# Local attention followed by a Fourier mix and an MLP: another load order, batch 1 on the later batches' path, batch 0's reversed copies taken from PSUM

## The chip, the cores and the metric

The kernel runs on one core of a Trainium2 chip. The metric is device time in microseconds (us); a run's time is that of the one core. The profile is one execution recorded by the hardware profiler. PE is TensorE (matmuls), PEld its weight loads, DVE is VectorE, ACT is ScalarE, POOL is GpSimd, SP is SyncE, whose queue issues most DMAs.

## The reference

Inputs are q, k, v of shape (4 batches, 8 heads, 768 positions, 64), and two weight matrices, 512 x 2048 and 2048 x 512, all float32. Cut to what matters:

```python
scores = q @ k^T / 8 + bias          # bias = -slope[h] * distance
keep   = (pos < 8) | (0 <= rel < 96) # 8 global columns, a local band of 96
a      = softmax(where(keep, scores, -1e9));  attn = a @ v
x      = attn.transpose(0, 2, 1, 3).reshape(4, 768, 512)
u      = x + real(fft(fft(x, axis=1), axis=2))
un     = (u - mean) / sqrt(var + 1e-6)
out    = u + relu(un @ w_ch1) @ w_ch2
```

## The kernel before

The four batches pass through the same stages; a head pair `hp` (two heads of 64, 128 lanes) is the unit of attention.

**Attention.** `load` brings q, k and v of a pair to SBUF as float32 (384 KB each). `cast_qk` or `cast_direct` makes them float16. `trans` turns q and k by TensorE transposes into a PSUM tile `pt` and evacuates it to `qkT` (L521); `trans_dma` does it by DMA transposes instead. `score` computes three groups `g` of score tiles per pair. In batches 0 and 1 a matmul of the constant distance table against a scaled identity `sid` (L542, L547) first puts the bias into the PSUM bank, the score matmuls (L552) are added to it, and ScalarE's exponential (L575) is the weight. In batches 2 and 3 there is no bias matmul: ScalarE writes the exponential to `er` (L572), and VectorE multiplies it by a table `mk` (L587), which ScalarE computes once from the distances (L1128). v takes two paths as well: in batches 0 and 1 it is cast (`cast_v0`, L414), and `v_place` permutes its rows with small matmuls (`pvp`, L427) and copies the result out of PSUM (L443, L444); in batches 2 and 3 the load itself permutes the rows (two DMAs, L336) and POOL casts once (`cast_v`, L454). `FB = 2` is the first batch of the later path. The eight global columns go through `kG` (small POOL copies of `qkT`, L481), `v_global`, `glob`, and `av` adds all into `pav`, which VectorE normalizes into `x` (L699, L700).

**Mix.** `bounce` writes `x` to DRAM and reads it back in another row order as `xr` (L719, L727). The Fourier transform is folded: sums and differences on VectorE (`fold_3` for batch 0, `fold_s` and `fold_d` for the others) into `zy`, `eA`, `ww`; then `y_unit` (matmuls `py`, L881; copies to `zy`, L896, L898), `mirror` (POOL copies of `zy` with reversed order, L916 to L918 into `rev`, L929 into `ww`), and `u_unit` (matmuls `pu`, L961; VectorE adds `xr` and accumulates the row sum, L980; L984 scales that sum; L995 and L997 normalize the mean away). `nt_unit` transposes the result (`ptu`, L1025) and copies it to `unT`. ScalarE's squares (L1004) and POOL's power (L1011, L1012) give the deviation.

**MLP.** Per chunk of 256 rows (12 chunks), `ph_unit` does eight groups of the first product (L1053) with a Relu to `hT` (L1059, L1060), and `pg_unit` the second product (L1076), whose result VectorE adds to `u` (L1085) before the store (L1090).

**The order of the work** comes from a planner, class `Plan`, which runs while the program is built. Each engine has a clock, each operation a cost in us, a list of what it needs and a rank. TensorE takes from four streams (`MIX`, `ATT`, `PH`, `PG`) the unit that can start first; `later` puts other operations in a list, and the one that can start first is written out, lower rank first. The engines run the queues so written in order.

**Buffers and gates.** `buf` hands out rotating SBUF tiles, and `free` names the release that the next user waits for. q and k of batch 1 are staged in the tiles of w1 and w2, so both weights load only when these casts are done: `wload` issues eight POOL DMAs (L1164, L1169), each a quarter of w1 or w2 with a cast to float16. `hold`, a 4-byte DMA on SP that reads the last quarter of w2 (L1178), holds back batch 2's loads. Batches 0 and 1 may use two more pairs of PSUM banks, `C` and `D`; `ph` and `pg` use that space afterwards, so `ph_unit` needs the token `CD`, given when all of batch 0's units with a choice of banks, and those of batch 1 that took `C` or `D`, are done:

```python
needs = [("unT", c), ("w1", jp // 2)] + (free("hT", 5 + c) if jp == 0 else []) + [("CD",)]
```

Of the kernel before, what the change touches and what calls it, by code (L numbers as in the profile page):

```python
# [14 lines left out]
P = 128  # L15


class Plan:
# [10 lines left out]
    def __init__(self):  # L29
        self.t = {"PE": 0.0, "ACT": 0.0, "DVE": 0.0, "POOL": 0.0, "SP": 0.7, "DMA": 1.9, "DMA2": 0.0}  # L30
        self.tok = {}
        self.ready = []
        self.pending = []
        self.rings = {}
        self.left = {}
        self.n = 0
# [49 lines left out]
    def emit(self, place):  # L86
# [6 lines left out]
        if dma:  # L93
            q = "DMA2" if eng == "ACT" or outs and outs[0][0] in ("xw", "xr") else "DMA"
# [82 lines left out]
def kernel(  # L177
# [23 lines left out]
    FB = 2  # L201
    DB = 1
    assert (B, H, S, Dh, NG, NL) == (4, 8, 768, 64, 8, 96)
# [66 lines left out]
    def bank(tag, name, dtype=FP32):  # L270
# [4 lines left out]
        if "late" not in early:  # L275
# [6 lines left out]
            "ww": 1, "rev0": 1, "u": 4, "un": 2, "unT": 2, "w1": 1, "w2": 1}  # L282
# [36 lines left out]

    def load(b, hp, which):  # L320
        n = HP * b + hp
        h0 = 2 * hp
        gate = [("gate",)] if n == FB * HP else []
        if b >= FB:
            srcs = [(0, q), (1, k)] if which == "qk" else [(2, v)]
            for w, src in srcs:
                i = 2 + 3 * (n - FB * HP) + w

                def run(src=src, i=i, w=w):
                    t = stage[("t", n, w)] = buf("qs", i, [P, 2 * NS, Dh], FP32, 1)  # L330
# [6 lines left out]
                pl.later([("SP", 0.55 if w < 2 else 1.1, run)], free("qs", i) + gate, 0.0, [("ld", n, w)], lat=1.7, dma=2.67)  # L337
                if w < 2:
                    cast_direct(b, hp, w, i)
# [5 lines left out]
        else:  # L345
            tag, ti, users, slot = (("hT", hp, 2, 0) if hp < 3 else ("qs", 0, 1, None)) if b == 0 else \
                (("w1", "w2")[hp // 2], 0, 4, 2 * (hp % 2))
            for w, src in enumerate((q, k)):
                at = (tag, ti) if slot is not None else (tag, w)

                def run(w=w, src=src, at=at):
                    if slot is None:
                        t = buf(at[0], at[1], [P, NS, 2 * Dh], FP32, 1)
                    else:
                        if at not in stage:
                            stage[at] = buf(at[0], at[1], [P, users, NS, 2 * Dh], FP32, users)
                        t = stage[at][:, slot + w]
                    stage[("t", n, w)] = t
# [16 lines left out]
    def cast_qk(b, hp, w, at):  # L375
# [9 lines left out]
        if b == 0 and not (w and hp):  # L385
            ways.append(("DVE", dve2(768), lambda: cast("DVE")))
        elif b == 0:
            ways = [("POOL", 0.87, lambda: cast("POOL"))]
        else:
            ways.append(("POOL", 0.87, lambda: cast("POOL")))  # L390
        pl.later(ways, [("ld", n, w)] + free("qk", n), 0.0, [("qk", n, w)], [("free",) + at], rank=b)

    def cast_direct(b, hp, w, i):
# [895 lines left out]
```

## Time and profile before

| what | before |
|---|---|
| time, median of 3 runs | 279.25 us (278.58 to 280.61) |
| the profiled execution's own time | 280.46 us |
| its span | 278.7 us |
| PE busy | 258.7 us, 93% |
| DVE busy | 157.9 us, 57% |
| ACT busy | 148.0 us, 53% |
| POOL busy | 60.8 us, 22% |
| mean granted clock of PE | 0.999 |
| read from and written to HBM | 31.92 MB, 9.44 MB |

The span is what the profile covers; the time of the same execution is 1.76 us longer. Busy time is that in which at least one instruction of the engine runs. Matmuls overlap, and the profile models their ends, so a busy PE need not be at its peak rate. In the timeline a line gives start, duration, engine, source line, operation, output<-input, count, and in brackets the idle time before it with what ended it.

### The profile page before, as it was taken

The page shows a single profiled execution, that of the slowest core. Times are in us where ns is not written, and L with a number is a line of the kernel's source. Part 1 is how long each engine was busy: PE and PEld are TensorE (multiplying, and loading weights), DVE is VectorE, ACT ScalarE, POOL GpSimd, SP SyncE. Part 2 cuts the span into 40 slices and gives each one's busy share as a digit, 9 for nine tenths or more (in the row PEclk, how much of TensorE's full clock was granted, in tenths as well). Part 3 has the DMA queues.
Part 4 walks back from the last instruction along what each step waited for, and adds up shares of the span by engine and source line. Part 5 has one row for each costly group of instructions (what it writes and reads, how often), then busy time and mean ns, then how long its engine had stood idle before and what let it go on. Part 6 is the DMA issues. An engine that isn't in the chain of part 4 may idle for free.

```text
span 278.7 us, 6005 instructions
## 1 busy us (share of the span) xinstructions
PE 258.7 (93%) x2448; PEld 173.2 (62%) x2448; DVE 157.9 (57%) x323; ACT 148.0 (53%) x255; POOL 60.8 (22%) x127
## 2 busy tenths in 40 slices
PE   1999789598789999999999999999999999999994
PEld 1445538458657874677486466777866677767441
DVE  4347781985786414766278968666896661111121
ACT  1466675495666642797782237889242256434000
POOL 1435365931002512412110021401001320100000
PEclk9999999999999999999999999999999999999999
DMA  7999999997774498978858895200164020110122
GB/s 206 290 291 257 339 304 196 207 204 119 194 204 144 105 167 162 231 137 165 196 146 196 214 263 104 66 2 0 40 136 168 1 78 1 40 38 22 56 75 75
DMA packets 70301, 40.69 MB, mean 146 GB/s; under 512 B 27394, under 2 KB 66306, under 8 KB 70274
## 3 DMA queue, kind: packets, MB, share of 16 engines
q1 hardware_dynamic: 61474, 29.83, 43.6%
q0 software_dynamic: 4224, 4.19, 9.3%
q10 hardware_dynamic: 4576, 6.29, 8.3%
q8 instruction: 19, 0.31, 0.5%
q14 instruction: 8, 0.07, 0.1%
HBM read 31.92 MB, written 9.44 MB: 148 GB/s over the span
## 4 chain that ended last, share of the span: by engine, by line
PE 81%; DVE 8%; ACT 4%; issue 2%; DMA 2%; POOL 1%; ACTq 1%; SPq 0%; DVEq 0%; POOLq 0%
PE pg L1076 29%; PE ph L1053 29%; PE py L881 5%; PE sc L552 4%; PE pav L680 3%; PE pu L961 3%; ACT ex L575 2%; PE pt L515 2%; DVE qkT L521 2%; PE ptu L1025 2%; DMA ident<-idm 2%; PE sc L547 2%; PE pav L669 1%; PE sc L542 1%; DVE sm L984 1%
## 5 line engine op out<-in xcount | busy, mean ns | idle before, releaser
L1053 PE MATMUL ph<-unT,w 128*128 128x256 f16 x768 | 93.8, 273 | 2.2 <-DVE hT L1060 2.2
L1076 PE MATMUL pg<-w,hT 128*128 128x512 f16 x384 | 89.9, 379 | 0.0
L1053 PEld LDWEIGHTS <-w 128*128 128x128 f16 x768 | 72.7, 98 | 18.4 <-issue 6.1
L1059 ACT ACTIVATE hT<-ph 128x512 f16<-128x512 f32 x73 | 43.6, 597 | 48.1 <-PE ph L1053 46.9
L1076 PEld LDWEIGHTS <-hT 128*128 128x128 f16 x384 | 36.8, 98 | 36.3 <-issue 0.4
L1085 DVE SCALAR_TENSOR_TENSOR u<-pg,sm,u 128x512 f32<-128x512 f32 x24 | 18.0, 750 | 53.7 <-PE pg L1076 53.5
L575 ACT ACTIVATE ex<-sc 128x992 f16<-128x992 f32 (+2 forms) x24 | 21.3, 925 | 15.1 <-PE sc L552 11.1
L1060 DVE TENSOR_SCALAR hT<-ph 128x512 f16<-128x512 f32 x23 | 15.9, 690 | 11.5 <-PE ph L1053 11.5
L572 ACT ACTIVATE er<-sc 128x992 f16<-128x992 f32 (+2 forms) x24 | 21.5, 923 | 1.6 <-PE sc L552 1.6
L1011 POOL TENSOR_SCALAR sm<-sm 128x2 f32<-128x2 f32 x12 | 3.2, 264 | 71.9 <-ACT un L1004 71.7
L929 POOL COPY ww<-zy 128x512 f16<-128x512 f16 x16 | 9.4, 613 | 42.4 <-PE py L881 42.4
L980 DVE SCALAR_TENSOR_TENSOR u<-pu,xr 128x512 f32<-128x512 f32 x24 | 15.6, 688 | 4.7 <-PE pu L961 4.0
L552 PE MATMUL sc<-qkT 64*128 64x256 f16 (+1 forms) x192 | 17.8, 275 | 0.2 <-DVE qkT L521 0.2
L369 ACT ACTIVATE qk<-qs 128x384 f16<-128x384 f32 (+1 forms) x31 | 14.5, 528 | 6.1 <-DMA qkT<-qk 4.8
L587 DVE TENSOR_TENSOR ex<-er,mk 128x992 f16<-128x992 f16 (+2 forms) x24 | 15.2, 645 | 3.8 <-ACT er L572 3.6
L995 ACT ACTIVATE un<-u,sm 128x512 f16<-128x512 f32 x12 | 8.5, 716 | 16.1 <-DVE sm L984 13.0
L680 PE MATMUL pav<-v,ex 128*128 128x65 f16 x352 | 16.4, 193 | 0.4 <-ACT ex L575 0.4
L680 PEld LDWEIGHTS <-ex 128*128 128x128 f16 x352 | 15.1, 97 | 1.8 <-issue 1.1
L552 PEld LDWEIGHTS <-qkT 64*128 64x128 f16 x192 | 6.0, 96 | 16.1 <-issue 13.2
L896 ACT ACTIVATE zy<-py 128x512 f16<-128x512 f32 (+1 forms) x10 | 8.1, 810 | 14.7 <-PE py L881 14.7
L1004 ACT ACTIVATE un<-un 128x512 f16<-128x512 f16 x24 | 14.8, 620 | 1.5 <-PE ptu L1025 1.4
L898 DVE CAST zy<-py 128x512 f16<-128x512 f32 (+1 forms) x9 | 8.3, 927 | 10.5 <-ACT zy L896 6.4
(101 smaller groups left out, 305.8 us busy)
## 6 DMA issues: line engine op xcount, KB each, us to landing
out_dram<-u SPq DMA_DIRECT2D x24, 256.0 KB, 2.2
w<-in_moe_w_ch_dram POOLq DMA_DIRECT2D x8, 512.0 KB, 11.8
qs<-in_q_dram SPq DMA_DIRECT2D x9, 384.0 KB, 4.7
qs<-in_k_dram SPq DMA_DIRECT2D x9, 384.0 KB, 5.4
u<-in_v_dram SPq DMA_DIRECT2D x8, 384.0 KB, 7.7
xr<-xd ACTq DMA_DIRECT2D x4, 768.0 KB, 4.3
qs<-in_v_dram SPq DMA_DIRECT2D x16, 192.0 KB, 3.9
w<-in_q_dram SPq DMA_DIRECT2D x4, 384.0 KB, 7.5
```

What stands on the lines that cost most here:

```text
L552: nc.tensor.matmul(pa[:, s, c0:c0 + cw], TT[n][lo:lo + 64, 1, i * P:(i + 1) * P], TT[n][lo:lo + 64, 0, i * P:i * P + cw], start=(b > 1), s ...
L572: A(mine(), cut(pa), AF.Exp, 0.0, 0.125)
L575: A(cut(expst[hp][:, :, g * 512:g * 512 + (384 if g == 2 else 512)]), cut(pa), AF.Exp, 0.0, 0.125)
L587: VT(o, mine(), m, op=ALU.mult)
L680: nc.tensor.matmul(po[:, jj, hh * 65:(hh + 1) * 65], lhsT, v16[b % 2][:, i, h, 0:65], start=(jp == 0 and a == 0), stop=(a == len(ops) - 1) ...
L980: V.scalar_tensor_tensor(u[:, a].rearrange("p (n r) -> p n r", r=4), pu[:, a].rearrange("p (r n) -> p n r", r=4), 1.0, XR[b][:, rr].rearra ...
L1004: A(x, x, AF.Square, accum_out=MV[c][:, a, 2:3])
L1053: nc.tensor.matmul(ph[:, a * CH:(a + 1) * CH], W1[0][:, d, jb * P:(jb + 1) * P], UNT[c][:, d, :], start=(d == 0), stop=(d == ND - 1))
L1059: pl.later([("ACT", act(512), lambda: A(dst, ph, AF.Relu)), ("DVE", dve(512), lambda: V.tensor_scalar_max(dst, ph, 0.0))], [], e, [("h", c ...
L1060: ("DVE", dve(512), lambda: V.tensor_scalar_max(dst, ph, 0.0))],
L1076: nc.tensor.matmul(pg, HT[c][:, jb, t * P:(t + 1) * P], W2[0][:, jb, :], start=(jb == 0), stop=(jb == NJ - 1))
L1085: V.scalar_tensor_tensor(UT[c][:, t, :], pg, MV[c][:, t, 3:4], UT[c][:, t, :], op0=ALU.mult, op1=ALU.add)
```

## The change

Batch 1 takes the path of batches 2 and 3 (`FB = 1`) for its v and its scores; its q and k are still transposed by TensorE (`PT`). The loads are ordered: batch 0, five loads of batch 1 (`EARLY`), w1, the rest of batch 1 after batch 0's bounce (token `xi`), then w2, whose tile stages q and k of batch 1's pairs 0 and 1. w1 waits for the cast of batch 1's first q (`W1AT`), its third quarter for the second write of the bounce. Batch 2's loads wait for the third quarter of w2 (`WG`) in place of the last. Batch 0's bounce is issued by SP. The tables `mk` are computed at the start. `kG` is copied from PSUM by the engine that evacuates `pt`, in batches 0 and 1. The reversed copies of batch 0 (`turn`) and the two special rows of every batch (`back`) are made from PSUM by ACT or DVE; POOL keeps the four larger copies of batches 1 to 3. Batch 0's scaling of the row sum goes from DVE to ACT. `C` and `D` are for batch 0 alone.

```diff
-    FB = 2
+    FB = 1
     DB = 1
+    WG = 2
+    W2AT = 1
+    MKA = 4
+    EARLY = [(4, 0), (4, 1), (4, 2), (5, 0), (5, 1)]
+    W1AT = ("qk", 4, 0)
+    PT = (0, 1, 2, 3)
...
+    order = [(n, w) for n in range(HP, B * HP) for w in range(3) if n >= HP + 2 or w == 2]
+    def place(n, w):
+        return ("qs", 2 + order.index((n, w))) if (n, w) in order else ("w2", 0)
...
-                pl.later([("SP", 0.55 if w < 2 else 1.1, run)], free("qs", i) + gate, 0.0, [("ld", n, w)], lat=1.7, dma=2.67)
+                pl.later([("SP", 0.55 if w < 2 else 1.1, run)], free(*at) + gate + [("xi",)] * (b == 1 and (n, w) not in EARLY), 0.0, [("ld", n, w)], lat=1.7, dma=1.47 if w < 2 else 2.3)
...
     def BANKS(b):
-        return ("xx", "C", "D") if b < 2 else ("xx",)
+        return ("xx", "C", "D") if b == 0 else ("xx",)
...
+    def kg_now(b, hp, on, pt):
+        for s in range(2):
+            c0 = 16 * (hp % 2) + 8 * s
+            d = kG[b % 2][64 * s:64 * s + 64, hp, c0:c0 + NG].rearrange("p (t m) -> p t m", t=2)
+            x = pt[64 * s:64 * s + 64, 1, 0:P].rearrange("p (t m) -> p t m", t=2)[:, :, 0:NG // 2]
+            copy_on(on, d, x)
...
-        if b >= FB:
+        if b > FB or b == FB and hp not in PT:
             return trans_dma(b, hp)
...
+            def evac(on):
+                TT[n] = buf("qkT", n, [P, 2, S], FP16, 4)
+                copy_on(on, TT[n], pt[:, :, 0:S])
+                kg_now(b, hp, on, pt)
...
-            if b < 2:
+            if b == 0:
                 for s in range(2):
                     lhsT = sid[:, 2 * hp + s, :]
...
-    XT = [("x", 0), ("hT", 4), ("x", 1), ("x", 2)]
+    XT = [("x", b) for b in range(B)]
...
-        on, eng = "ACT", nc.scalar
+        on, eng = ("ACT", nc.scalar) if b else ("SP", nc.sync)
...
+            def back(on):
+                d = T[("y", b)][:, 7]
+                s0 = py[:, 0, :].rearrange("p (a c m) -> p a c m", a=2, c=2)
+                copy_on(on, d[:, 0, :, 0:1], s0[:, 0, :, 0:1])
+                copy_on(on, d[:, 0, :, 1:P], s0[:, 0, :, P - 1:0:-1])
+                copy_on(on, d[:, 1], s0[:, 1, :, ::-1])
...
+            def turn(on, t):
+                d = REV[0][:, 2 * g + t]
+                copy_on(on, d.rearrange("p a c m -> p (a c) m"), py[:, t, :].rearrange("p (x m) -> p x m", m=P)[:, :, ::-1])
...
-                V.tensor_scalar_mul(sm[:, :, 1], sm[:, :, 0], -SC / Dm)
+                if b:
+                    V.tensor_scalar_mul(sm[:, :, 1], sm[:, :, 0], -SC / Dm)
+                else:
+                    A(sm[:, :, 1], sm[:, :, 0], AF.Copy, 0.0, -SC / Dm)
...
-            pl.later([("ACT", 2 * act(NM), m)], [("c", "dist"), ("x", 1, 3, 2)], 0.0, [("mk", hp)], rank=3)
+            pl.later([("ACT", 2 * act(NM), m)], [("c", "dist")] + [("ex", 0, 3, 2)] * (hp >= MKA), 0.0, [("mk", hp)], rank=2)
...
-            needs = [("vc", 5), ("free", "w1", 0)] if i == 0 else [("wl", 3), ("free", "w2", 0)] if i == 4 else [("wl", i - 1)]
+            needs = [W1AT] if i == 0 else [("wl", 3), ("free", "w2", 0), ("v", 1, W2AT)] if i == 4 else [("wl", i - 1)] + [("xw", 0, 1)] * (i == 2)
...
-            nc.sync.dma_start(g, W2[0][0:1, NJ - 1, 0:2])
-        pl.later([("SP", 0.45, hold)], [("w2", 3)], 0.0, [("gate",)])
+            nc.sync.dma_start(g, W2[0][0:1, 4 * WG, 0:2])
+        pl.later([("SP", 0.45, hold)], [("w2", WG)], 0.0, [("gate",)])
...
-                    if b == 1:
-                        v_place(b, hp)
...
-            mirror(b)
+            if b >= DB:
+                mirror(b)
```

## The prediction

> **What bounds the kernel now.** I read the page's busy line and its 40 slices first, then the busy time of the engines in four stretches that I cut at events of TensorE (PE): its first matmul (6.17), the first score of batch 1 (33.41), the first `ph` matmul (64.33), the end of the last visible wait (98).
>
> ```profile
> PE 258.7 (93%) x2448; PEld 173.2 (62%) x2448; DVE 157.9 (57%) x323; ACT 148.0 (53%) x255; POOL 60.8 (22%) x127
> ...
> PE   1999789598789999999999999999999999999994
> ```
> ```profile
> 6.17:33.41 27.24, 25.07 (x301) 13.00 (x302) 15.89 (x40) 16.19 (x21) 10.91 (x21) 1.00 1.14 290
> 33.41:64.33 30.92, 25.90 (x339) 17.10 (x337) 22.45 (x47) 21.40 (x36) 19.28 (x31) 1.00 1.13 235
> 64.33:98.00 33.67, 31.05 (x324) 25.46 (x321) 21.12 (x40) 20.77 (x39) 5.51 (x10) 1.00 0.62 153
> 98.00:274.70 176.70, 176.67 (x1498) 117.69 (x1496) 95.44 (x185) 88.36 (x159) 24.08 (x57) 1.00 0.46 107
> ```
>
> Columns: stretch, its length, busy PE, PEld, DVE, ACT, POOL, clock, DMA, GB/s. From 98 on PE has no gap, and the clock is full. So the 278.7 us are 6.2 us before the first matmul, 258.7 of PE work, a tail of 4.0 after 274.7, and three idle sums: 2.2, 5.0 and 2.6 (9.8 together). The end moves only by PE work removed or by these 9.8 us growing or shrinking. The second stretch matters most; its PE timeline:
>
> ```profile
> 37.61 0.58 PE L547 MATMUL sc<-dist,sid 128*128 128x496 f16 x2
> 38.12 0.39 PE L552 MATMUL sc<-qkT 64*128 64x256 f16 x4
> ...
> 49.64 0.53 PE L427 MATMUL pvp<-er,ident 64*64 64x128 f16 x24
> ...
> 54.75 0.62 PE L1025 MATMUL ptu<-ident,un 128*128 128x128 f16 x8 [2.50 <-ACT un L995]
> ...
> 60.32 1.07 PE L961 MATMUL pu<-t,ww 128*128 128x128 f16 x16
> ...
> 64.33 1.03 PE L1053 MATMUL ph<-unT,w 128*128 128x256 f16 x8
> ```
>
> The reader is to see that batch 0's last `pu` runs at 60.32, 11.7 us after its last `py` matmul (48.66). `ph` may start only when that `pu` has left its PSUM bank. DVE and POOL say why it is so late:
>
> ```profile
> 51.16 2.78 DVE L984 TENSOR_SCALAR sm<-sm 128x2 f32<-128x2 f32 x1
> ```
> ```profile
> 53.84 0.92 POOL L1169 DMA_DIRECT2D w<-in_moe_w_ch_dram x1
> 54.76 0.84 POOL L414 CAST er<-u 128x768 f16<-128x768 f32 x1
> 55.53 0.62 POOL L929 COPY ww<-zy 128x512 f16<-128x512 f16 x1
> ```
>
> A 2-element operation took 2.78 us while POOL issued w2 and copied (11 others: 0.17), and POOL's reversed copies stood behind weight issues and casts.
>
> **The change, part by part.**
>
> *PE work removed.* Batch 1 loses its bias matmuls. One head pair's three run from 37.61 to 38.12, 38.44 to 38.95 and 39.74 to 40.16: 0.51 + 0.51 + 0.42 = 1.44 us, four pairs 5.8. Lower bound by streaming alone: 2 x (496 + 480 + 384) columns at the rate of `ph` (8 x 256 columns in 0.87 us, 0.425 ns a column) is 1.16, four pairs 4.6. I take 5.8, because batch 2's score without bias takes 0.31 to its successor (122.40 to 122.72), as the plain part does here. `v_place` of batch 1 goes: 0.46 + 0.29 + 0.29 = 1.0. Transposes stay on PE. Sum: 6.8 (5.6 at least), PE work 251.9.
>
> *What comes ahead of the first `ph`.* All 6.8 us lay before 64.33, where PE had 25.07 + 25.90 = 51.0 us of work; 44.2 are left. The removed work was also filler while batch 0's chain ran elsewhere, so it pays only if `ph` moves up. Earliest start T: the last x ends at 34.95; folds until 38.82; 60 `py` matmuls of 0.111 us (6.6) until 45.5. Then three `pu` and three pairs of u additions (6 x 0.69 on DVE from 1.15 us after the last `py`), 5.7 us to the last: T = 51.2. This needs the reversed copies by then. They go to ACT and DVE, straight from PSUM: four of 512 elements (nearest row, the straight copy L898, 0.69; POOL needed 0.61 from SBUF; if reversed reading doubled it, 1.4) and `back` (row L700, 256 elements 0.42, twice, plus a small one: 1.0). Batch 0's scaling L984 goes to ACT, about 0.2 us (nearest row there, 128x1, 0.19), out of POOL's way.
>
> *DVE's additions before T.* Twelve multiplications by `mk` at 0.645 (row L587, 128x992 etc.): 7.7. Sixteen small `kG` copies from PSUM: not in the trace; between 0.06 (a 128x1 memset) and 0.37 (L609 on ACT, 32x256), I take 0.16 as of L1151 (32x4 from PSUM): 2.6. Turns 2.8, `back` 1.0. Removed: four L443 (0.63) 2.5, three L984 0.5. Net 11.1 if DVE takes everything. In 33 to 64 DVE was idle 30.9 - 22.5 = 8.5 us, in 6 to 33 11.4, and ACT shares copies and turns. Cover exists, but a started multiplication holds batch 0's next step up to 0.65. I charge 2 of the 11.1; bounds 0 and 11.1.
>
> *ACT.* The eight `mk` exponentials (0.67 apart) move from 74 to the start: 5.4 us into a stretch where ACT idles 11.0. Each pair can hold one score's exponential by 1.3 at most, and PSUM has banks in reserve. Batch 0's bounce leaves ACT's queue: issues of 1.88, 1.26 and 0.35, of which 1.18 stood on the chain of waits at 27.42. Batch 1's casts become two of 0.518 for one of 0.845: at most 8 x 0.19 = 1.5. Together I charge +0.8 (bounds -1.2 and +4). So T = 51.2 + 2 + 0.8 = 54.0.
>
> *Queues.* SP gets the bounce's five DMAs. Its xr read waits there for the write to land (5.8 us median), and behind it stand seven loads of batch 1 (ten DMAs, since a v is two): from about 35 + 1.3 + 5.8 + 0.4 = 42.5, against 37 before. At 290 GB/s their 2.75 MB take 9.5 us, the second half of w1 beside them two chunks of 2.6 (512 KB at the 204 GB/s of that stage): landed by about 57. Pairs 2 and 3 of batch 1 wait for that, and with them its global part and av. POOL's third w1 issue waits for the bounce too, and its casts of batch 1 stand behind it. Half of w1 is issued at about 26 and needs up to 13 us; the other half by 55.5, when `ph` needs it at T + 3.5. w2 follows by about 67.5 (69.5 before), covered by 24 `ph` groups x 0.87 = 20.9 us from T. The four v loads of batch 1 turn from one 384 KB DMA into two of 192 KB; SP's two issues of such a v took between 1.3 and 4.6 us (L336), a plain one 0.4 to 2.6. Nothing on SP before 64 is nearer than that to PE; it is in the 57.
>
> The Trainium skill, "DMA: Bandwidth & Descriptors", "Why small descriptors are slow (HBM only)", puts the loss at 256-byte descriptors at 27%, which speaks against this v path: by it the four loads would take an estimated 1.5 us more of DMA time, and T or the filler would be that much later at worst. The trace has such loads only in a quiet stage (landing 3.9 us), so no row shows it.
>
> *Weight issues against DVE.* Row: L984 lost 2.6 us to a run of POOL work with four issues, 0.65 each. Chunks 0 to 3 now stand in batch 0's stage: 0 to 2.6, inside the charge of 2 above.
>
> The Trainium skill, "SBUF — State Buffer", "Who interferes with whom", says that GpSimd and a DVE instruction in a two-port mode exclude each other for a whole instruction. It speaks against w1 beside batch 0's attention; by it and the 0.75 us of an issue the estimate would be 4 x 0.75 = 3.0, and the forecast 0.4 later.
>
> *Sum.* Work that can be late: of the 44.2, pairs 2 and 3 (two transposes 1.35, six scores 1.8, global 0.7, av 1.9) = 5.7. So PE has done W = 38.5 to 44.2 at T; middle 41.4. Idle before `ph`: 54.0 - 6.2 - 41.4 = 6.4, against 7.2 now. After it I keep 2.6. Span: 6.2 + 251.9 + 6.4 + 2.6 + 4.0 = 271.1. The profiled execution took 280.46, its span and 1.76 around it; the median of the runs is 279.25, the span and 0.55. So 271.1 + 0.55 = **271.6**. From 98 on, batches 2 and 3 are untouched and I charge nothing: PE is covered there by backlog; if that were gone, each missing us would count fully.
>
> **Rivals.**
> *No pay-off:* filler leaves, data of batch 1 come late, `ph` starts at 60. Idle 60 - 6.2 - 41.4 = 12.4; span 277.1, time 277.6. For it: SP's wait and 235 GB/s in that stretch. Against: w1 no longer waits for batch 1.
> *Full gain:* T near 52 with all 44.2 done leaves the 2.2 of the first stretch, and 0.7 later: 265.0, time 265.5. For it: each larger wait there has a cause that the change touches. Against: late loads.
> *Slower:* DVE becomes the bound of the head. All 11.1 stand before batch 0's steps, T = 62.3, and as batch 1 waits in the same line W is 38.5: idle 17.6, span 282.3, time 282.8. It is slower from T = W + 20.2 on (58.7 here), where the extra idle eats the 6.8. For it: DVE had 11.4 of 14 us busy from 28 to 42. Against: 8.5 idle us after 33, and ACT as a second taker.
>
> **How the numbers follow.** Forecast 0.60 (its own range 267 to 276: T = 52 with W = 44.2, where the first stretch's 2.2 remain, to T = 58 with W = 41.4), no pay-off 0.17, full gain 0.12, slower 0.11. The range runs from T = 51.2 with W = 44.2 and no later idle (264.8) to just past no pay-off, 278.5. About 1%, so 276.5 to 282, is what a measurement tells from no change. Faster: 0.58 of the forecast, the 0.12, and 0.03 of no pay-off, 0.73. Within 1%: 0.02, 0.14 and 0.01 of the slower case, 0.17. Slower: 0.10.
>
> **What would show it.** Right: no L547 or L542 in batch 1, PE busy near 252, first `ph` near 54, last `pu` of batch 0 within 4 us of its last `py`, no DVE operation of 2 elements near 3 us before it. Wrong: PE busy above 254, first `ph` after 58, a new wait of PE above 2 us for a load of batch 1, for `mk` or for a multiplication, or gaps after 98.

## The result and the profile after

The changed kernel takes 293.25 us in the median of four runs (292.73 to 293.70), against 278.91 us of the kernel before on the same chip (278.48 to 280.61). The ratio is 1.0502, with a 95% interval of 1.0451 to 1.0552: **5% slower, 14.3 us**, where the prediction said 271.6 us and at most 278.5. (Ratios here and below leave out runs more than 1.5% above the fastest of the same kernel, in e16 three of five and in e14 two of four, the profiled ones among them, so a ratio can be lower than that of the medians.) The profiled execution took 293.7 us, its span is 291.9 us, 13.2 more than before.

From the profile's page, the busy line of the engines, TensorE's 40 slices and its granted clock:

```profile
PE 259.9 (89%) x2376; PEld 173.1 (59%) x2376; DVE 167.3 (57%) x350; ACT 151.8 (52%) x277; POOL 45.8 (16%) x90
...
PE   1899589651999995899999999999999999999994
...
PEclk9999969895799999999999999999999999999999
```

TensorE has 72 matmuls fewer, and yet its busy time grew from 258.7 to 259.9 us. The clock row says why: some slices stand at 5 to 8 tenths. The windows view of the changed kernel, cut at its first `ph` (56.09), the end of the wait after it (72.50), and the two ends of the thin stretch after 100 (columns as in the prediction):

```profile
5.96:34.45 28.49, 25.05 (x301) 13.02 (x302) 17.78 (x55) 20.76 (x32) 9.19 (x11) 1.00 1.20 282
34.45:56.09 21.64, 16.52 (x176) 12.93 (x177) 16.75 (x37) 16.37 (x32) 4.80 (x7) 0.84 0.95 194
56.09:72.50 16.41, 7.31 (x61) 5.63 (x59) 4.28 (x9) 4.51 (x11) 1.75 (x3) 0.71 1.19 209
72.50:105.00 32.50, 32.50 (x327) 23.91 (x326) 25.48 (x47) 23.90 (x46) 6.28 (x10) 0.94 0.86 184
105.00:126.00 21.00, 17.02 (x157) 11.67 (x156) 11.09 (x24) 11.28 (x24) 6.54 (x13) 1.00 1.02 201
126.00:288.00 162.00, 161.51 (x1365) 105.97 (x1363) 89.30 (x173) 73.68 (x136) 16.24 (x39) 1.00 0.33 83
```

Length less PE busy gives TensorE's idle time: 3.4 and 5.1 us before the first `ph`, 9.1 in the third stretch, 4.0 in the fifth, 0.5 after. In the third stretch ScalarE, VectorE and TensorE are idle together (4.5, 4.3 and 7.3 busy us of 16.4), while the DMA engines are busy all along: everything waits for loads. Three lines of TensorE's timeline:

```profile
56.09 3.46 PE L1082 MATMUL ph<-unT,w 128*128 128x256 f16 x16
59.83 1.91 PE L1082 MATMUL ph<-unT,w 128*128 128x256 f16 x16
...
71.61 3.57 PE L1082 MATMUL ph<-unT,w 128*128 128x256 f16 x16 [9.10 <-ACT hT L1088]
```

The same sixteen matmuls take 1.91 us at full clock and about 3.5 at half. The bracket names what ended the wait of 9.10 us: a copy of `hT` on ScalarE. But a Relu of 0.6 us can't be late by itself, and the chain of waits over this stretch (start, duration, what) shows what stood ahead of it:

```profile
47.00 6.75 DMA qs<-in_k_dram
53.75 16.36 DMA qs<-in_q_dram
70.11 0.02 issue
70.14 0.94 ACT qk L382 x2
71.07 0.49 ACT hT L1088
71.56 0.04 issue
71.61 3.57 PE ph L1082 x16
```

The load of q of batch 1's pair 3, issued at 53.75, landed 16.36 us later. Its cast had been put into ScalarE's queue ahead of the evacuation of `ph`, and ScalarE took its queue in order: the `ph` matmuls that this copy evacuates had ended by 61.8, and the copy came at 70.98, right behind the cast. TensorE stood behind that evacuation. The last loads of batch 1 landed later still: k of pair 3 at about 72.6, and its V was cast at 74.48.

The load was issued so late for two reasons. One is in SyncE's waits (line, waited for, us in total, times, longest), the other in the timelines of SyncE and POOL:

```profile
SPq L742 <- DMA xd<-x: 8.1, 1, 8.1
```

```profile
47.00 2.15 SPq L378 DMA_DIRECT2D qs<-in_k_dram  x1
52.35 1.31 SPq L354 DMA_DIRECT2D qs<-in_v_dram  x2
53.75 0.60 SPq L378 DMA_DIRECT2D qs<-in_q_dram  x1
```

```profile
51.49 0.83 POOL L464 CAST v<-qs 128x768 f16<-128x768 f32 x1 [15.98 <-DMA qs<-in_v_dram]
```

SyncE holds the read of the bounce (L742) for 8.1 us until the write has landed, and q and k of pairs 2 and 3, with V from pair 1 on, stand behind it; in the kernel before all eight q and k loads of batch 1 were issued by 28 us. And in the changed kernel the loads behind the bounce share three rotating `qs` tiles. V of pair 2 uses the tile of pair 1's V, so its issue at 52.35 waited 3.1 us until that V had landed and POOL had cast it, and pair 3's q stood behind it in the queue. The kernel before had a place for each q and k in the tiles of w1 and w2.

**The account.** Clock loss is the sum, over windows of one us, of busy time times one less the granted clock; busy time less that is the work at full clock. This split is rough: the eleven kernels below with the same 2376 matmuls show between 248.6 and 253.7 us of work by it.

| us | before | after | difference |
|---|---|---|---|
| ahead of the first matmul | 6.2 | 6.0 | -0.2 |
| PE work at full clock | 258.7 | 253.3 | -5.4 |
| clock loss | 0.0 | 6.6 | +6.6 |
| idle between first and last matmul | 9.8 | 21.9 | +12.0 |
| tail | 4.0 | 4.2 | +0.2 |
| span | 278.7 | 291.9 | +13.2 |

So the work went away nearly as forecast, as far as this split can tell, and 18.6 us of idle time and half clock came in its place.

### The profile page after: what moved, and what is told of

The parts are those of the page before. It is cut to its first block, busy times and chain, and to the rows that moved or that the text cites. A ratio compares the mean times of both kernels' runs of the same rounds, so it can differ in the third digit from the quotient of the medians.

```text
span 291.9 us, 5881 instructions
## 1 busy us (share of the span) xinstructions
PE 259.9 (89%) x2376; PEld 173.1 (59%) x2376; DVE 167.3 (57%) x350; ACT 151.8 (52%) x277; POOL 45.8 (16%) x90
## 4 chain that ended last, share of the span: by engine, by line
PE 67%; DMA 18%; ACT 5%; DVE 5%; SPq 2%; issue 1%; ACTq 0%; DVEq 0%
PE ph L1082 27%; PE pg L1105 24%; DMA qs<-in_q_dram 8%; DMA xd<-x 5%; PE sc L567 3%; PE pav L695 3%; DMA qs<-in_k_dram 2%; PE py L897 2%; PE pu L992 2%; PE pt L529 2%; DVE x L715 2%; DMA dist<-distm 2%; DMA out_dram<-u 1%; PE ptu L1054 1%; ACT qk L382 1%
## 5 line engine op out<-in xcount | busy, mean ns | idle before, releaser
L1082 PE MATMUL ph<-unT,w 128*128 128x256 f16 x768 | 97.5, 279 | 9.2 <-ACT hT L1088 9.1
L587 ACT ACTIVATE er<-sc 128x992 f16<-128x992 f32 (+2 forms) x36 | 32.9, 923 | 8.8 <-PE sc L567 6.3
L1089 DVE TENSOR_SCALAR hT<-ph 128x512 f16<-128x512 f32 x25 | 17.2, 690 | 22.7 <-PE ph L1082 22.7
L602 DVE TENSOR_TENSOR ex<-er,mk 128x992 f16<-128x992 f16 (+2 forms) x36 | 23.8, 662 | 8.8 <-ACT er L587 8.8
L382 ACT ACTIVATE qk<-qs 128x384 f16<-128x384 f32 x38 | 17.5, 517 | 16.6 <-DMA qs<-in_q_dram 15.3
L464 POOL CAST v<-qs 128x768 f16<-128x768 f32 x12 | 10.2, 849 | 74.4 <-DMA qs<-in_v_dram 71.1
L567 PE MATMUL sc<-qkT 64*128 64x256 f16 (+1 forms) x192 | 18.5, 277 | 1.6 <-DVE x L715 1.4
L715 DVE TENSOR_TENSOR x<-pav,rc 128x512 f16<-128x512 f32 (+1 forms) x27 | 17.1, 632 | 0.9
L695 PE MATMUL pav<-v,ex 128*128 128x65 f16 x352 | 16.5, 194 | 0.4 <-ACT er L587 0.3
L1033 ACT ACTIVATE un<-un 128x512 f16<-128x512 f16 x24 | 14.8, 620 | 1.3 <-PE ptu L1054 1.2
L529 PE MATMUL pt<-ident,qk 128*128 128x128 f16 x96 | 9.1, 266 | 4.8 <-ACT er L587 2.0
L960 POOL COPY ww<-zy 128x512 f16<-128x512 f16 x12 | 7.0, 610 | 40.5 <-PE py L897 39.7
L1064 DVE COPY unT<-ptu 128x1024 f16<-128x1024 f16 x11 | 7.6, 690 | 9.5 <-PE ptu L1054 8.9
```

Of the source, the lines that this page charges most:

```text
L382: A(d, s, AF.Copy)
L567: nc.tensor.matmul(pa[:, s, c0:c0 + cw], TT[n][lo:lo + 64, 1, i * P:(i + 1) * P], TT[n][lo:lo + 64, 0, i * P:i * P + cw], start=(b > 0), s ...
L587: A(mine(), cut(pa), AF.Exp, 0.0, 0.125)
L602: VT(o, mine(), m, op=ALU.mult)
L695: nc.tensor.matmul(po[:, jj, hh * 65:(hh + 1) * 65], lhsT, v16[b % 2][:, i, h, 0:65], start=(jp == 0 and a == 0), stop=(a == len(ops) - 1) ...
L715: VT(X[b][:, 2 * jp:2 * jp + 2, first * Dh:(first + nh) * Dh].rearrange("p j (h d) -> p j h d", d=Dh), pv[:, :, :, 0:Dh], rc.to_broadcast( ...
```

## The experiments

The theories, by the letters that the expectations use. **A**: a cast that waits for a late load stands at the head of ScalarE's queue, and batch 0's steps behind it. **B**: the data of batch 1 are late, whoever casts them. **C**: work added to VectorE and ScalarE is the bound. **D**: the order of the loads makes the loss. **E**: batch 1's bias matmuls were filler, and without them TensorE idles and loses its clock. **W**: TensorE's sum of work decides.

All runs, with the ledger of each profiled execution in us (idle is that between the first and the last matmul):

| run | base | median | ratio to before [95%] | idle | clock loss |
|---|---|---|---|---|---|
| before | | 278.91 | 1 | 9.8 | 0.0 |
| after | | 293.25 | 1.050 [1.045, 1.055] | 21.9 | 6.6 |
| e1_pool_casts | after | 297.35 | 1.069 [1.062, 1.075] | 26.6 | 6.7 |
| e2_plan_costs | after | 291.69 | 1.046 [1.041, 1.050] | 21.5 | 9.7 |
| e3_w2_late | after | 290.77 | 1.045 [1.039, 1.050] | 21.0 | 6.1 |
| e4_early_all | after | 308.44 | 1.109 [1.105, 1.112] | 37.5 | 7.9 |
| e8_w1_last | after | 291.10 | 1.041 [1.036, 1.045] | 20.4 | 8.2 |
| e9_bounce_act | after | 302.38 | 1.079 [1.072, 1.086] | 27.9 | 14.9 |
| e14_mended | after | 293.81 | 1.043 [1.037, 1.048] | 21.4 | 13.2 |
| e11_after_filler | after | 295.74 | 1.061 [1.054, 1.068] | 23.2 | 5.1 |
| e5_bias_out | before | 290.79 | 1.039 [1.036, 1.042] | 18.5 | 10.3 |
| e6_pool_part | before | 280.07 | 1.002 [0.998, 1.005] | 9.2 | 1.5 |
| e7_both | e5 and e6 | 282.00 | 1.008 [1.006, 1.011] | 14.9 | 5.1 |
| e10_both_filler | e7 | 284.44 | 1.018 [1.012, 1.024] | 12.1 | 4.5 |
| e12_both_v | e7 | 280.59 | 1.006 [1.003, 1.010] | 14.0 | 4.0 |
| e13_both_banks | e7 | 284.19 | 1.016 [1.007, 1.026] | 14.3 | 6.6 |
| e15_pool_v | e6 | 281.07 | 1.004 [1.000, 1.008] | 9.7 | 4.7 |
| e16_held | e12 | 290.87 | 1.033 [1.027, 1.040] | 24.8 | 5.0 |
| e17_filler_held | e15 | 294.15 | 1.055 [1.051, 1.059] | 20.7 | 5.3 |
| e18_held_pool | e16 | 291.50 | 1.045 [1.039, 1.050] | 23.1 | 3.8 |

### First, single links of the changed kernel

**e1_pool_casts** takes the late casts out of ScalarE's queue.

```diff
-        pl.later([("ACT", act(768), lambda: cast("ACT")), ("POOL", 1.6, lambda: cast("POOL"))],
+        ways = [("ACT", act(768), lambda: cast("ACT")), ("POOL", 1.6, lambda: cast("POOL"))]
+        pl.later(ways[1:] if b == 1 and hp > 1 else ways,
```

> The changed kernel, but the casts of q and k of batch 1's pairs 2 and 3 can only go to POOL. Theory A (a late load's cast stands in ScalarE's in-order queue ahead of the Relu copies that free the ph banks): ScalarE's 10.0 us wait for a load of q and PE's 9.1 us wait for hT are gone, the clock stays full there, and of 293.3 us some 6 to 9 go: 284 to 287. Theory B (the late data itself starves PE, whichever engine waits for it): PE still has a gap of 7 us or more between 60 and 75, time 290 to 294. Theory C (VectorE's added work is the bound): no change, 293.

297.35 us, slower still and above all three ranges. The wait of 9.1 us is gone; from the timeline of TensorE in this kernel, the largest one near it:

```profile
72.00 0.29 PE L530 MATMUL pt<-ident,qk 128*128 128x128 f16 x1 [4.46 <-POOL qk L386]
```

Now TensorE waits for the same data one step later, at the transposes, and its idle time has grown by 4.7 us in all. Theory A named the place of the wait; its cause lies elsewhere.

**e2_plan_costs** gives the planner the transfer costs of the kernel before, with the weights on the account of the other loads.

```diff
-            q = "DMAW" if eng == "POOL" else "DMA2" if eng == "ACT" or ...
+            q = "DMA2" if eng == "ACT" or ...
-    ... lat=1.7, dma=1.47 if w < 2 else 2.3)      # loads
+    ... lat=1.7, dma=2.67)
-    ... lat=2.2, dma=2.6, rank=0                  # weights
+    ... lat=2.2, dma=3.3, rank=0
```

> The changed kernel, but the planner's costs of transfers as before: weight loads run on the same planned DMA clock as the other loads, a load costs 2.67 us, a weight chunk 3.3. No instruction's content changes, only order. Theory A (the order of ScalarE's queue was made with loads believed early): the casts of batch 1's pair 3 move behind the Relus of the ph groups, the 9.1 us gap goes, time 282 to 287. Theory B: the data comes as late as now and PE starves all the same, 290 to 294. Theory C: no change.

**e3_w2_late** moves w2's four chunks from 52 to 65 us, out of the way of pair 3's loads.

```diff
-    W2AT = 1
+    W2AT = 3
```

> The changed kernel, but w2's loads wait for the cast of pair 3's v instead of pair 1's, so that they don't run beside batch 1's last loads. If w2 makes these loads late (part of A, and B too): q of pair 3 lands about 58 instead of 70, the 9.1 us gap shrinks below 3, time 284 to 289, with the first pg later by up to 10 us. If the wait for the bounce on SP's queue alone makes them late: landing after 66, time 291 to 294.

291.69 and 290.77 us. In both the gap between 60 and 100 is gone and the medians are 1.6 and 2.5 us lower, no more; their ratios (1.046 and 1.045) are not clear of the changed kernel's 1.050. In e2 the half clock spreads over 30 to 60 us (loss 9.7), and TensorE is idle for 7.6 us after 100; in e3 it is idle for 7.25 us at one stroke, up to 110.70, because the backlog of `ph` and `pg` is used up before batch 1's mix is ready. What is late in batch 1 stays late; only the place changes at which TensorE runs out of other work.

**e4_early_all** issues all loads of batch 1 early, ahead of the bounce.

```diff
-    EARLY = [(4, 0), (4, 1), (4, 2), (5, 0), (5, 1)]
+    EARLY = [(n, w) for n in range(4, 8) for w in range(3)]
```

> The changed kernel, but none of batch 1's loads waits for batch 0's bounce. If the hold behind the bounce makes them late: they land up to 8 us earlier (the wait of SP from 36 to 44.5 is no longer ahead of them), the 9.1 us gap goes, time 284 to 289, with xr and the first ph up to 4 us later. If the collision with w2 alone makes them late: landing near 66 to 70 as now, time 291 to 295.

308.44 us, the worst. The read of the bounce was issued at 44.99 us, as in the changed kernel (44.50), but it landed 14.8 us later instead of 4.6, for w1's second half, three chunks of w2 and pair 3's q and k were all issued between 40.9 and 49.9. VectorE waited 8.36 us for it, the k load took 22.6 us, and the first `ph` came at 77.24. Loads that are merely early crowd out the one that batch 0 needs.

**e8_w1_last** turns the order back as far as these tiles allow: all loads early, the bounce on ScalarE's queue, w1 after batch 1's last load, w2 later.

```diff
-    EARLY = [(4, 0), (4, 1), (4, 2), (5, 0), (5, 1)]
-    W1AT = ("qk", 4, 0)
-    W2AT = 1
+    EARLY = [(n, w) for n in range(4, 8) for w in range(3)]
+    W1AT = ("ld", 7, 1)
+    W2AT = 3
...
-        on, eng = ("ACT", nc.scalar) if b else ("SP", nc.sync)
+        on, eng = "ACT", nc.scalar
```

> The changed kernel with the load order turned back as far as its buffers allow: no load of batch 1 waits for the bounce, which goes on ACT's queue again, w1 starts when pair 3's k has landed, w2 after pair 3's v. Theory D: batch 1's data lands by 50 and its mix is no longer late, the gaps from 60 on go, time 276 to 284, although the first ph is later (60 to 66). If not the order but the path (direct v loads, three staging buffers) makes batch 1 late: 288 to 295. Theory C: 290 or more.

**e9_bounce_act** moves batch 0's bounce to ScalarE's queue and nothing else (the last pair of lines above).

> The changed kernel with batch 0's trip of x through DRAM on ScalarE's queue instead of SyncE's, nothing else. If the hold of SyncE's queue from 36 to 44 us is what makes pair 3 of batch 1 late (D), q of pair 3 lands by about 62 instead of 70, the gap of 9.1 us shrinks to under 4, and the time is 286 to 289. If the transfers themselves are what is late (B), issuing them sooner moves nothing: 291 to 294, the gap stays above 7.

**e14_mended** mends three links together: the bounce on ScalarE's queue, `W2AT = 3`, and the PSUM rings for batch 1.

```diff
-        return ("xx", "C", "D") if b == 0 else ("xx",)
+        return ("xx", "C", "D") if b < 2 else ("xx",)
```

> The changed kernel with three links of its order mended together: batch 0's trip of x through DRAM is issued on ScalarE's queue again, so that the loads of batch 1 on SyncE's queue stand behind no wait for it; w2 waits for its later place (this alone gave -2.5 us); and batch 1 may again use the PSUM rings C and D as before (taking them away cost 2.2 us on the other base). Theory D (each link of the order has its own price and they add up): -2.5, -2.2 and some -3 for the hold of SyncE's queue, so 284 to 287 us, with no gap over 3 us in TensorE's row between 60 and 100. Theory A in its later form (the links trade one wait for another, because batch 1's work is late as a whole and TensorE has nothing else): 289 to 292, the idle time between 65 and 130 still over 6 us.

291.10, 302.38 and 293.81 us. In e9 pair 2's q was issued at 31.23 instead of 46.32, but pair 3's only at 69.20 instead of 53.75: w2's chunks went out at 50.41, the V load beside them took until 68, and SyncE waited 16.5 us for the tile that it filled. That V load had itself waited for pair 1's V, which was issued at 28.95 beside w1's chunks and cast at 49.65. The time lies above both ranges of the expectation. In e8 nothing of batch 1 stands behind the bounce, and it still lies 4.1% above the kernel before: the three tiles let pair 3's q out only at 41.49 (26.23 before), and its V, issued at 44.80 beside w1's chunks, was cast at 60.10. So the hold is not the only thing in the new order that costs. Within the changed kernel's buffers no order that was tried recovers more than a fifth of the loss; the prices do not add as theory D in its simple form said (284 to 287 for e14). What had to be tried was the other direction: one part at a time on the kernel before.

### Second, parts of the change on the kernel before

**e6_pool_part** is the part that takes Pool's copies of batch 0 (and the `kG` copies) away, all from PSUM by other engines, with the scaling on ScalarE.

```diff
+    def kg_now(b, hp, on, pt): ...          # kG from PSUM, by the engine that evacuates pt
+            def back(on): ...               # reversed rows from PSUM, ACT or DVE
+            def turn(on, t): ...
-            mirror(b)
+            if b >= DB:
+                mirror(b)
```

> The kernel before with another part alone: batch 0's reversed copies and every batch's two special rows from PSUM by ACT or DVE, kG from PSUM by the evacuating engine, batch 0's row sum scaled on ACT. Theory D: the last pu of batch 0 moves from 60 to about 52, the first ph from 64 to 56 to 60, the 2.5 us wait goes, PE work stays 258.7, time 274 to 278. Theory C: the copies delay DVE and ACT as much as they spare POOL, 278 to 282.

**e5_bias_out** gives batch 1's scores the path of the later batches: no bias matmuls, `mk` at the start.

```diff
-            if b < 2:
+            if b == 0:                      # bias matmuls, exponential straight to expst
-        ... [("c", "dist"), ("x", 1, 3, 2)], 0.0, [("mk", hp)], rank=3)
+        ... [("c", "dist")], 0.0, [("mk", hp)], rank=2)
```

> The kernel before with one part of the change: batch 1's scores take the later path (no bias matmuls, multiplication by mk, mk at the start); loads, v, bounce and POOL's copies as before, and an own buffer for the cast v. Theory D (the load order costs the time: w1 ahead of half of batch 1 makes batch 1's data, attention and mix late, and PE runs dry before 65 and again after 100): 5.8 us of PE work go at a place where data is there, PE busy 253, time 273 to 277. Theory C (VectorE's and ScalarE's added work in the head costs it): 279 to 285.

**e7_both** is e5 and e6 together.

> The kernel before with both parts, so nearly the whole change without its load order, its v path and its bounce on SP. Theory D: the sum of both, PE busy 252 to 253, no half clock, time 268 to 273. Theory C: both delays add up, 282 or more.

280.07, 290.79 and 282.00 us. The Pool part makes no difference that can be measured (ratio 0.998 to 1.005), although its first `ph` stands at 58.60 instead of 64.33: TensorE had the same work in another order. The bias path alone costs 3.9%; TensorE waits up to 3.50 us there for POOL's reversed `ww`. With both, 24 matmuls are gone (251.1 us of work at full clock, 256.7 in e6) and the time is 0.8% longer. None of the three came out in the range of theory D; e6 and e7 lie in that of theory C, and e5 lies above it. The timeline of e7 shows idle time and half clock in the place of the work:

```profile
57.02 1.87 PE L1047 MATMUL ptu<-ident,un 128*128 128x128 f16 x16 [3.22 <-DVE v L443]
...
60.71 2.99 PE L1075 MATMUL ph<-unT,w 128*128 128x256 f16 x16
```

So in the head, up to the first `ph`, the later path as a whole wins no time, and theory W, by which its 5 us or more of PE work would all be won, does not hold. VectorE was busy for 40.0 and ScalarE for 36.3 of the 55.0 us before e7's first `ph`, so neither is full, but TensorE's waits there end on copies and exponentials of these two.

**e10_both_filler** and **e11_after_filler** issue batch 1's bias matmuls again as useless work on e7 and on the changed kernel; the score matmuls overwrite them.

```diff
-            if b == 0:
+            if b < 2:
...
-                         start=True, stop=False, skip_group_check=True)
+                         start=True, stop=(b > 0), skip_group_check=True)
```

> The run with both parts of the change on the kernel before (e7), and batch 1's bias matmuls issued again as useless work: the score matmuls overwrite what they leave, the path with mk stays, and the order of every queue stays. Theory E (the bias matmuls were filler in a stretch where data and evacuations set the pace; without them PE idles, and its clock is granted at half for some us): 5.8 us of useless PE work cost nothing, clock loss falls from 5.1 us to under 2, visible idle between 6 and 65 falls from 13.2 to about 8, time 278 to 282 (282.0 without). Theory W (PE's work sums up wherever it lies): 286 to 289.

> The changed kernel with the same useless matmuls in batch 1's scores. Theory E: clock loss from 6.6 us to about 4, since a part of the slow clock comes from the 9 us gap after 62, which stays; time 290 to 294 (293.3 without). Theory W: 297 to 300.

284.44 us, 2.4 more than e7, and 295.74, 2.5 more than the changed kernel. By the ledgers the 5.4 us of work added in e10 were met by 2.8 us less idle time and 0.7 less clock loss. So theory E is right in that idle time was there to be filled, and wrong in that filling it brings the kernel back: the time is longer, not shorter. By the ratios, the useless work costs 1.0% (0.3 to 1.7), about half of its 5.4 us.

e10 also prices the other side of the path, for it and e6 issue the same 2448 matmuls. What differs is batch 1's path through `er` and `mk`, above all twelve multiplications on VectorE (busy for 169.1 us instead of 159.4), `mk` at the start, and an own buffer for the cast v, and the order that the planner makes of this. The ratio goes from 1.002 to 1.018, 1.6% (0.9 to 2.4). So a smaller form of theory C holds here: the later path costs about 4.5 us, and the removed bias matmuls give back some 2.7 of it.

**e12_both_v** loads batch 1's V straight into its layout on e7; **e13_both_banks** takes the rings C and D from batch 1 on e7; **e15_pool_v** is e6 with that V path and with batch 1's bias matmuls kept.

```diff
+                if b:                       # e12, e15: two loads of 192 KB, cast once on POOL
+                    x = v[b, h0:h0 + 2].rearrange("h s d -> (h s) d").rearrange("(n m t) d -> t m n d", m=64, t=2)
...
-        return ("xx", "C", "D") if b < 2 else ("xx",)
+        return ("xx", "C", "D") if b == 0 else ("xx",)          # e13
```

> e7 with batch 1's v loaded directly in its final row order (two DMAs of 192 KB in place of one of 384, 256-byte runs) and cast by POOL, v_place of batch 1 gone; the order of the loads stays. If the direct v loads make the head's transfers late (L, a part of what separates e7 from the changed kernel): weights land 1 to 3 us later and time is 284 to 288. If it is neutral or a gain (1.0 us of PE work and eight evacuations less): 279 to 283.

> e7 with batch 1 kept off the PSUM banks C and D, as in the changed kernel. If two banks are too few for batch 1's scores (B): more waits of PE for evacuations between 31 and 60, time 284 to 290. If banks don't matter: 280 to 283.

> The kernel before with two parts of the change that cost nothing by themselves, and no others: Pool's copies of batch 0 given to other engines, and batch 1's V loaded straight into its layout and cast on GpSimd, with no placing matmuls (some 1 us of TensorE's work). Batch 1's bias matmuls stay, so TensorE keeps its filler. By theory E (the filler is what keeps the stretch whole): 276 to 279, and a clock loss under 2 us. By theory W (TensorE's sum decides, wherever work goes): e6 less 1 us, 278 to 280, and later than the version without the bias matmuls by their 5.8 us of work if that sum decided, so that version should have been the faster one: against W already. If the v loads' short runs cost: over 281.

280.59, 284.19 and 281.07 us. The V path costs nothing that can be seen (0.6% against e7's 0.8%). The banks may cost 0.8%, 2.2 us by the medians, but this is not clear of noise: the intervals overlap (1.007 to 1.026 against 1.006 to 1.011). e15 missed theory E's 276 to 279 and its clock loss under 2 us (4.7). And e12 against e15 compares the later score path as a whole with the earlier one: 249.6 against 254.0 us of PE work at full clock, 14.0 against 9.7 us idle, the same time. This idle time does not come from the missing matmuls alone: from e6 to e10 (path added) it grows by 2.9 us, from e10 to e7 (matmuls gone) by 2.8.

### Third, the hold alone

**e16_held** puts one thing of the changed order on e12, whose buffers are those of the kernel before: the bounce on SyncE's queue, with the loads of batch 1 that the change holds behind it.

```diff
+    EARLY = [(4, 0), (4, 1), (4, 2), (5, 0), (5, 1)]
...
-        on, eng = "ACT", nc.scalar
+        on, eng = ("ACT", nc.scalar) if b else ("SP", nc.sync)
...
-                pl.later([("SP", 0.55, run)], free(*at), 0.0, ...
+                pl.later([("SP", 0.55, run)], free(*at) + [("xi",)] * (b == 1 and (n, w) not in EARLY), 0.0, ...
```

> The version with batch 1 on the later path, V loaded directly and the kernel before's buffers (280.6 us), with one thing of the changed order put on it: batch 0's trip of x through DRAM goes on SyncE's queue, and the loads of batch 1 that the change holds (pairs 2 and 3, V of pair 1 on) stand behind it, so q and k are issued near 45 to 55 us instead of by 28. Theory D (the hold makes batch 1 late, and that is the changed kernel's loss): +7 to +11, 287 to 292 us, a gap of over 3 us in TensorE's row or half clock past 60. Rival S (it is the staging buffers shared with later batches and the early w1 that cost, the hold is covered by the 128 ph matmuls from 58 us): within 2 us of it, 279 to 283.

**e17_filler_held** puts the same on e15, which keeps the bias matmuls.

> The same hold on the version that keeps batch 1's bias matmuls (281.1 us without the hold). Theory E (the filler is TensorE's own work only while batch 1's data are there: a bias matmul opens a score group that waits for the same transposes, so it covers nothing of late loads): as much loss as without the filler, +7 to +11, 288 to 292. If the filler does cover late loads, the loss is smaller by its 5.8 us: +2 to +5, 283 to 286.

290.87 us against 280.59, by the ratios 1.0334 / 1.0064 = 2.7% or 7.5 us; and 294.15 against 281.07, 5.1% or 14 us. The hold costs what theory D said, with no other edit of the new order: on e12 2.7% with an interval of 1.9 to 3.5, on e15 even more, so bias matmuls cover nothing of it. One thing moves along: the weights wait for casts of held loads, so w1's first chunk is issued at 45.78 instead of 41.83 and w2's at 65.65 instead of 48.88; no wait of TensorE up to 130 us ends on a weight load. The profile of e16 repeats the picture of the changed kernel. ScalarE, then TensorE:

```profile
58.49 0.84 ACT L376 ACTIVATE qk<-w 128x768 f16<-128x768 f32 x1 [4.94 <-DMA w<-in_q_dram]
...
64.27 0.84 ACT L376 ACTIVATE qk<-w 128x768 f16<-128x768 f32 x1 [4.32 <-DMA w<-in_k_dram]
```

```profile
66.78 1.01 PE L1054 MATMUL ptu<-ident,un 128*128 128x128 f16 x8 [10.59 <-ACT unT L1062]
```

ScalarE waits twice for loads at the head of its queue, and TensorE 10.59 us for a copy behind them. Where the lateness comes from is in the last column of the windows view, GB/s moved, between 30 and 40 us. First e12, then e16:

```profile
30.00:35.00 5.00, 3.12 (x64) 2.83 (x64) 4.24 (x13) 1.62 (x2) 1.61 (x2) 1.00 1.16 329
35.00:40.00 5.00, 2.64 (x36) 1.76 (x37) 4.86 (x10) 2.87 (x5) 1.89 (x3) 0.94 1.13 202
```

```profile
30.00:35.00 5.00, 3.17 (x71) 2.85 (x68) 3.91 (x15) 1.42 (x3) 0.83 (x1) 1.00 0.51 102
35.00:40.00 5.00, 2.86 (x33) 1.91 (x31) 4.92 (x11) 4.28 (x6) 0.00 (x0) 0.92 0.51 117
```

While SyncE's queue waits, the DMA engines work at half: (329 - 102 + 202 - 117) x 5 us is 1,560 KB that are not moved. They are moved later; at the 210 GB/s that e16 moves between 45 and 50 us, beside w1, they take an estimated 7.4 us. That agrees with the 7.5 us of the ratios; it is a sum that fits, not a second measurement.

**e18_held_pool** is e16 with the casts of pairs 2 and 3 on POOL alone, theory A on a base where nothing but the hold is there.

```diff
+        elif hp > 1:
+            ways = [("POOL", 0.87, lambda: cast("POOL"))]
```

> The held version (290.9 us; without the hold 280.6) with the casts of pairs 2 and 3 of batch 1 on GpSimd alone, so that no late load's cast can stand at the head of ScalarE's queue. In the held version ScalarE waited for such loads from 53.5 to 57.6 and from 59.9 to 64.3 us, and TensorE waited 10.6 us for a transposed copy queued behind. Theory A (the late load costs through ScalarE's queue, where batch 0's steps stand behind the cast): the wait of 10.6 us goes and does not come back elsewhere, 281 to 285 us. Theory B (the lateness of the data itself costs, whoever casts): the wait moves to batch 1's transposes or later, 287 to 292.

291.50 us, no gain (1.045 against 1.033). From TensorE's timeline:

```profile
60.54 0.82 PE L531 MATMUL pt<-ident,qk 128*128 128x128 f16 x6 [2.42 <-POOL qk L380]
...
67.54 0.27 PE L615 MATMUL pvg<-v,ident 128*32 128x64 f16 x2 [5.85 <-POOL v L463]
```

The wait of 10.59 us is now one of 2.42 for the late q or k and one of 5.85 for the late V. Theory B holds and A falls: ScalarE's queue is where the lateness showed, not what made it dear. In e17, too, TensorE waits 5.31 us for a late k's cast and 4.93 for a late V's, both on POOL.

**Sum of causes.** The path of batch 1 and the Pool part, without their banks (e12): 0.6%. Banks (e13 over e7): 0.8%. The hold (e16 over e12): 2.7%. Multiplied, 1.042, of the 1.050 measured. This is a sum that nearly fits, not a proof. The banks' part is not clear of noise, the hold costs 5.1% on e15, and within the changed kernel taking the hold away did not bring the time back (e8 1.041, e9 1.079). What is shown is that holding batch 1's loads costs 2.7% or more on the old buffers, and that in the changed kernel TensorE stands behind late loads. How its loss divides among the hold, the three shared `qs` tiles and the weights' transfers amid batch 1's loads stays open, for the last two were not tried alone. No version that ran beats the kernel before.

## Why the prediction was wrong, step by step

**PE work removed: right.** Forecast 251.9 us, found 253.3 at full clock, and 248.6 to 253.7 in the other runs with the same matmuls. No bias matmul of batch 1 and no `pvp` of it is left.

**What comes ahead of the first `ph`: nearly right.** T was given as 54.0 and is 56.09; the last `pu` of batch 0 came within 4 us of its last `py`, VectorE's 2.78 us stall at L984 is gone, and a `kG` copy took 0.16 us as taken. The idle time before it is 8.6 us instead of 6.4. The charge of 2 us for VectorE's additions fits T, but e10 over e6 puts the path with its multiplications at 4.5 us of the whole time.

**Queues: the step that failed.** The prediction saw that ten DMAs of batch 1 stand behind the bounce's wait on SyncE, and then set them to have "landed by about 57". Pair 3's q landed at 70, its k at about 72.6, and its V was cast at 74.48. Two things were left out of that term. It let them all issue in a row after 42.5, though they share three tiles, each of which a cast must first release: pair 2's V was issued at 52.35, pair 3's k at 54.78 and its V, which waited for the cast of pair 2's, at 66.42. And it let w2 off with "covered by 24 `ph` groups x 0.87 = 20.9 us" without asking what w2 does to the loads: its four chunks were issued at 52.26, beside pair 3's, whose q then took 16.36 us.

**The cover after T: the step that made it dear.** "After it I keep 2.6": measured 13.3 us. The 24 groups of `ph` need ScalarE's evacuations and batch 0's other steps, which stand in queues with batch 1's casts; and what TensorE uses up of its backlog while batch 1 is late is missing again at 110. e3, e1 and e18 show this: each mended wait came back at the next place.

**The clock: a term that wasn't there.** That "the clock is full" was read from a kernel whose longest gap after the first matmul was 2.5 us, and the sum has no term for the clock. 6.6 us went here. With the 1.4 us of work, the four differences, 2.2 + 10.7 + 6.6 + 1.4 = 20.9, make up the 20.8 us between 271.1 and the span of 291.9 (start and tail cancel to 0.1).

**The rivals.** "No pay-off" had the right mechanism (filler leaves, batch 1's data come late behind SP's wait), but ended it at the first `ph`, priced at 277.6; e7 and e12, which have the filler's part of it without the late loads, came out at 282.0 and 280.6. The slower rival, VectorE as the bound of the head, did not happen: T came at 56.09, and between 63 and 70 us VectorE did nothing. As the account of the whole loss theory C falls with it; that VectorE's added work has a price stands, by e10 over e6. Of the signs named as wrong, three came: PE busy above 254 (259.9, by the slow clock), a wait of TensorE above 2 us behind a load of batch 1, and the gaps after 98.

**The two cited rules.** The Trainium skill's 27% for 256-byte descriptors ("DMA: Bandwidth & Descriptors", "Why small descriptors are slow (HBM only)"), an estimated 1.5 us for the V loads, shows as no loss: e12 is 1.4 us faster than e7 by the medians, with intervals that overlap. But e12 also drops `v_place`, so a loss of that size could be hidden. The exclusion that the Trainium skill states in "SBUF — State Buffer", "Who interferes with whom", was put at 0.4 us; no run here separates it.

## What to carry to other kernels

Price a load that is moved behind a wait by the bytes that the DMA engines do not move during the wait, and ask what those bytes meet when they are moved at last; where a tile is reused, the load also waits for the consumer of the one before it. Work taken from TensorE in a stretch that loads and evacuations pace is only partly won (about half here), and the work that another engine takes over for it has its own price there (1.6% here). An idle stretch of some 3 us more can also cost half the clock for 4 to 5 us. The engine named as ending a wait is the messenger: follow its queue back to what stood ahead, and test by the opposite direction (one part put on the old kernel), since mending single links of the new one mostly moved the wait.

## What the runs showed of the hardware

**Half clock after thin stretches, not only after empty ones.** By the windows view, the granted clock of the changed kernel fell to 0.50 at about 35.4, 55.9 and 66.1 us. Ahead of the third fall TensorE was idle from 62.5 on, 3.6 us; ahead of the first two it was busy for some 1.6 and 1.7 of the last 3.4 us. The clock came back about 4.8, 3.7 and 4.7 us after TensorE was busy without a break. The kernel before was busy for only 0.9 of the 3.4 us from 52 and kept its full clock, so these rows give no threshold. The Trainium skill, "TensorE: Matmul & The Clock Gate", "Part 1: The HAM clock gate (the "warmup" mystery)", gives windows of about 3.4 us for both turns, which run freely. The third fall agrees, the returns took a little longer than one such window, and the first two falls came after stretches that were not idle but busy by half.

**A load beside the weights took two to five times its usual time.** The median landing of the q loads into `qs` was 4.4 us in the changed kernel; the one issued among w2's four chunks of 512 KB took 16.36. In e16 a k load beside w1's took 16.30 (7.8 in the median of batch 1's four), and in e4 one amid five chunks 22.6 (4.6 in the median of its k loads).
